# Quarter products for six gated blocks of an attention, gated layer and softmax-linear-unit kernel

## The chip, the cores and the metric

The kernel runs on one core of a Trainium2 chip. The core has engines that work beside each other, each through its own queue in program order: TensorE (PE; its weight loads are listed apart as PEld), VectorE (DVE), ScalarE (ACT), GpSimd (POOL) and SyncE (SP), which here issues nearly all transfers between the device memory and the on-chip memory. An engine waits for another through semaphores. The metric is device time of one execution in microseconds (us), the median of several runs.

## The reference

```python
def _moe_ref(x, w1, w2, w3, w_out):          # x: 1792 tokens x 768, from attention
    a = x @ w1                               # 768 x 1024
    b = x @ w2
    h = a * b @ w3                           # 1024 x 1024
    return (h @ w_out).astype(np.float32)    # 1024 x 768

def _moe2_ref(x, w_in, w_out, g_ln):
    h = x @ w_in                             # 768 x 1024
    e = np.exp(h - np.max(h, axis=-1, keepdims=True))
    sm = e / (np.sum(e, axis=-1, keepdims=True) + 1e-09)
    solu = h * sm
    ln = (solu - mean(solu)) / np.sqrt(var(solu) + 1e-06) * g_ln
    return (ln @ w_out).astype(np.float32)   # 1024 x 768
```

Ahead of these stands attention over 4 sequences, 12 heads, 448 positions of width 64, whose scores are capped by a tanh. Its output, laid out as 1792 tokens of width 768, is the x of the gated layer.

## The kernel before

Numbers are held as two parts, a high one and a low one of reduced precision, and each product is made as three (`THREE`: high by high, high by low, low by high). Splitting a tile means a cast on ScalarE for the high part ("a<-s", "ws<-ws" in the rows) and a subtraction on VectorE for the low part.

The work has three stages. Attention goes over 24 pairs of heads. Beside it run the folding of weights (w3, w_out and w_in are multiplied into one matrix W of 1024 x 1024, since nothing stands between them) and the first gated blocks. The gated stage makes, for each block f of 128 of the 1024 columns of w1 and w2 and each of the four sequences b (448 tokens), two banks of 128 x 448 with 6 x 3 matmuls each (L981); one is copied by ScalarE (L338), and VectorE multiplies the other with it (`evict`, L1002) into "abs", which SyncE stores (`ab_dr`). It goes in two passes: all eight blocks for sequences 0 and 1, then all eight for sequences 2 and 3 (`PASSES`). For the second pass six of the eight blocks' weights are fetched again, 1.5 MB each (`plan_again`, L790, "wt<-w_dr"), from a copy in the device memory.

Stage 3 multiplies the gated result with W in seven rounds of two token tiles, takes the softmax-like part, and multiplies with wout2 in seven more. Each round is one Strassen-Winograd step: with halves of both operands, seven products (`product`, L1202; order 1, 2, 6, 7, 5, 4, 3) instead of eight, each of 12 matmuls of 512 columns (384 for wout2). Products 1, 6, 5 and 3 go to a bank "u", 2 to "y", 7 and 4 to "v"; 6 starts anew in "u", 5 and 3 add to it, 4 adds to "v". Between them the banks are copied by ScalarE (`kept`, L1206: "p", "u") or summed by VectorE (`added`, L1228). The operands of the products are sums of quarters ("s", "a0_1" to "a0_7" for round 0) and of W's quarters ("ws1" to "ws7"), whose sums are formed on VectorE in the gated stage (`plan_sums`, L866 to L869: "t") and stored (`tw_dr`, `tg_dr` for wout2).

What sets the order: up to the end of the gated stage a planner (`Order`, `Ahead`) places the work beside TensorE's by costs written into each step and by the order in which items were planned; wout2's conversions (`plan_last`: L326, L329, L332 on VectorE, the gain L910 on ScalarE, a store) were planned behind the first pass's blocks. In stage 3 the order is written out: `plan(r, j, ...)` lists what stands behind product j of round r. Either way each engine then runs its list in order. `first_operands` (L962, L963) makes the operands of stage 3's first products in the second pass.

Of the kernel before, what the change touches and what calls it, by code (L numbers as in the profile page):

```python
# [18 lines left out]
P = 128  # L19
# [13 lines left out]
PLAIN, XR, LEAN = 6, 5, 1000.0  # L33
# [208 lines left out]
def attention_moe_solu(ctx: ExitStack, tc: tile.TileContext, q, k, v, cap, w12, w3t, wo, win, wout2, g_ln, out):  # L242
# [40 lines left out]
    right, left = [], []  # L283
    at = opened(right, "at", "right")
# [221 lines left out]

    def values(n):
# [127 lines left out]

    STAGE1, HALFWAY = 4 * NC * NF * 3, NC * NF * 3
# [123 lines left out]
    wt, xs, rb, fin = {}, {}, {}, set()  # L760
# [5 lines left out]
    def slot12(f, i):  # L766
        if i == 0:
            p = place["wt"] if f >= NF and (f - NF) % 3 == 2 else res[0]
            wt[f] = p.tile([P, 2, 2 * DM], F32R, tag="wres", bufs=1 if p is not res[0] else 2, name=f"wt{f}")
        return wt[f][:, 0, i * HALF:(i + 1) * HALF], wt[f][:, 1, i * HALF:(i + 1) * HALF]  # L770

    def free12(f):

        if f == NF + 2:
            return "wt" in place
        before = f - 2 if f < NF + 2 else f - 3
        return pos[0] >= STAGE1 and (f < 2 or (before, PASSES[before // NF][-1]) in fin)
# [8 lines left out]
    def plan_again(f):  # L786
        def load():
            for i in range(3):
                slot12(f, i)
            sync.dma_start(out=raw(wt[f]), in_=w12_dr[block(f)])  # L790
        for i in range(3):
            ahead.add(("w", f, i), load if i == 0 else (lambda: None), list, list, None, there12(f))

    def place_x(b, c):

        n = b * NC + c
        if n < W3 or n >= 2 * W3:
            return w3p.tile([P, 2, HALF], F32R, tag="w3", bufs=W3, name=f"xs{b}_{c}")[:, :, :S]
        return place["x"].tile([P, 2, S], F32R, tag="xs", bufs=W3, name=f"xs{b}_{c}")

    def free_x(b, part):
        if b == 0:
            return pos[0] >= STAGE1 + (HALFWAY if part else 0)
        return (pos[0] >= STAGE1 + HALFWAY if (b, part) == (1, 0) else "x" in place) and (b < 3 or (NF - 1, 0) in fin)

    def plan_x(b, parts=range(NPAIR // 2)):
        for part in parts:
# [17 lines left out]
            def scale(i=i, part=part, one=one):  # L825
                dve.scalar_tensor_tensor(xr[b, part], xr[b, part], one[0], rb.pop(i), ALU.mult, ALU.mult)
# [4 lines left out]
            def rest(part=part):  # L831
                x, steps = xr.pop((b, part)), []
                for i in range(2):
                    to = xs[b, 2 * part + i]
                    steps.append(("any", 1, copying(S), None, lambda e, to=to, i=i: cast(to[:, 0], x[:, i], e)))
                for i in range(2):
                    to = xs[b, 2 * part + i]
                    steps.append(("dve", 2, 560, 680, lambda to=to, i=i: low(to[:, 0], to[:, 1], x[:, i])))
# [19 lines left out]

    def plan_sums(kind, dr, t_dr, i_, part, n):
# [3 lines left out]
        def rest():  # L863
            b = lands.pop(i).rearrange("p (g h n) -> p g h n", g=2, h=2)
            t = [place["ts"].tile([P, HALF], F32, tag="ts", bufs=5, name=f"t{i}_{m}")[:, :2 * n].rearrange("p (t n) -> p t n", t=2) for m in range(2)]
            dve.tensor_tensor(t[0][:, 0], b[:, 0, 1], b[:, 0, 0], ALU.subtract)  # L866
            dve.tensor_tensor(t[0][:, 1], b[:, 1, 1], t[0][:, 0], ALU.subtract)
            dve.tensor_tensor(t[1][:, 0], b[:, 1, 1], b[:, 0, 1], ALU.subtract)
            dve.tensor_tensor(t[1][:, 1], b[:, 1, 0], t[0][:, 1], ALU.subtract)  # L869
            for m in range(2):  # L870
                sync.dma_start(out=t_dr[2 * m:2 * m + 2, :, i_, part * n:(part + 1) * n].rearrange("t p n -> p t n"), in_=t[m])
# [20 lines left out]
    def fifth(m):  # L892
        if m not in place["ws"]:
            close(right, 1)
            place["w5"] = opened(right, "ws5", "right")
            place["ws"][m] = place["w5"].tile([P, 2, NF // 2, HALF], F32R, tag=f"w{m}", name=f"ws{m}")
        return place["ws"][m]

    def plan_block(m, part):
        there = since((lambda: "ws" in place) if m != EARLY[4] else (lambda: (NF + 5, PASSES[1][1]) in fin and ("tg", NF // 2 - 1, 1) in ahead.done))  # L900
        ahead.add(("f", m, part), lambda: block_load(m, part, W4, tw_dr, fifth(m)), list,
                  lambda: [("none", 0, 0, 0, lambda: block_split(ws[m], part))], None, there)

    def plan_last(f):
        for u in range(2):
            i, slots, t = len(ahead.items), [], []

            def gain(i=i, t=t):
                t.append(early.tile([P, DM // 2], F32, tag="wg", bufs=2, name=f"wg{f}_{u}"))
                act.activation(t[0], cvs.pop(i), AF.Copy, scale=gt[:, f:f + 1])  # L910

            def rest(slots=slots, gain=gain, u=u, t=t):
                return [("act", 1, 460, 640, gain), ("none", 0, 0, 0, lambda: ring["cv"].give(slots[0], order.time)), ("sp", 0, 450, 5000, lambda: sync.dma_start(out=wg_dr[f, u], in_=t[0]))]
            ahead.add(("g", f, u), lambda i=i, u=u: landing(i, wout2[f, u].bitcast(U32), DM, U32), lambda i=i, slots=slots: convert(i, DM // 2, slots), rest, lambda: ring["cv"].when() if order.live else 0.0, None, ("sp", 450, 6000))
# [12 lines left out]
    plan_again(NF + 2)  # L927
# [3 lines left out]
    for f in range(NF):  # L931
        if f >= 3:
            plan_again(NF + f)
        if f < 4:
            for part in range(2):
                plan_block(EARLY[f], part)
    for i_ in range(NF // 2):
        for part in range(2):
            plan_sums("tg", G4, tg_dr, i_, part, DM // 4)
    for part in range(2):  # L940
        plan_block(EARLY[4], part)
# [23 lines left out]
    ahead.add("a0", load_first, list, lambda: [("none", 0, 0, 0, first_operands)], None, since(lambda: (NF + 2, PASSES[1][0]) in fin))  # L965

    def gated():
        pp = {}

        def products(f, b, cs):  # L970
            at_ = f - 2 if f in (NF, NF + 1) else f
            for i in range(2):
                for c in cs:
                    for m, (u, e) in enumerate(THREE):
                        begins = c == 0 and m == 0
                        yield 201, [("w", at_, (i * NC + c) // 4), ("x", b, c // 2), *(bank("f") if begins else [])]
                        if begins:
                            tag = "o" if "ws" in place and (i if b < 3 or f >= NF + 2 else f % 2) else "f"
# [7 lines left out]
            if cs[-1] < NC - 1:  # L986
                return
# [380 lines left out]
    def load_wg(m):  # L1368
        wg[m] = (wsp if m in EARLY[:4] else place["w5"] if m in EARLY else wsl).tile([P, 2, NF // 2, HALF], F32R, tag=f"w{m}", name=f"wg{m}")[:, :, :, :DM // 2]
        block_load(m, None, G4, tg_dr, wg[m])  # L1370

    def parts(t, part):
        return (t[:, i, rows(part), :] for i in range(2))

    def high_w(t, m, part=None):
        hi, lo = parts(t[m], part)
        act.copy(hi, raw(lo))

    def low_w(t, m, part=None):
        hi, lo = parts(t[m], part)  # L1380
        dve.tensor_tensor(lo, raw(lo), raw(hi), ALU.subtract)  # L1381

    def plan(r, j, *entries):
        for f, *args in entries:
            side.setdefault((r, j), []).append(lambda f=f, args=args: f(*args))
# [9 lines left out]

    plan(0, 0, (load_late, 4), (load_late, 3), (load, 1, 0), (load, 1, 1), (begun_sums,))
    plan(0, 1, (high, 0, 7))
    plan(0, 2, (high, 0, 5), (low, 0, 7), (high_w, ws, 4, 0))
    plan(0, 3, (high, 0, 4), (sum4, 0), (low, 0, 5), (low_w, ws, 4, 0), (high_w, ws, 4, 1))
# [125 lines left out]
```

## Time and profile before

| | us |
|---|---|
| median of 3 runs (785.34 to 785.66) | 785.48 |
| the profiled execution | 786.16 |
| its span, first to last instruction | 784.4 |
| TensorE busy in it | 777.3 |
| VectorE busy | 551.5 |
| ScalarE busy | 422.5 |
| GpSimd busy | 54.5 |

The rows further below are of the profiled execution. "Idle before" a row is the time in which its engine stood, and the name behind the arrow is what ended it. The chain of waits follows the work that ended last back to the start; where it runs on TensorE without a gap, TensorE sets the time there. "Landing" of a transfer is from its issue to its end. The granted clock is TensorE's, as a share of full speed; it is 1.000 over the span.

### The profile page before, as it was taken

What the parts mean: (1) busy time and instruction counts of PE and PEld (TensorE: products, weight loads), DVE (VectorE), ACT (ScalarE), POOL (GpSimd) and SP (SyncE); (2) the same over time, 40 slices, a digit from 0 to 9 for tenths busy, and PEclk for the clock granted to TensorE, in tenths of its full rate; (3) what the DMA queues carried; (4) which work ended last, traced back from release to release, by engine and by line L of the source; (5) the groups of instructions that cost most, each with busy time, mean ns of one, the idle gap of its engine ahead of it and who ended that gap; (6) DMA issues with size and microseconds to landing.
All of it is one profiled execution on the core that took longest, in us unless ns stands there. A gap on an engine that the chain in (4) does not pass through costs nothing.

```text
span 784.4 us, 11179 instructions
## 1 busy us (share of the span) xinstructions
PE 777.3 (99%) x4010; PEld 621.2 (79%) x4010; DVE 551.5 (70%) x998; ACT 422.5 (54%) x614; POOL 54.5 (7%) x106
## 2 busy tenths in 40 slices
PE   9999999999999999999999999999999999999998
PEld 6556666876856676767999999998788888999998
DVE  6896695789984478955785743441886668978972
ACT  6786767347467866672332311121576666845642
POOL 0111000100110111100000000000011111100000
PEclk9999999999999999999999999999999999999999
DMA  8867375677972374738888999962553345997332
GB/s 288 248 222 233 115 230 160 191 246 245 295 245 80 104 256 157 247 140 306 323 279 229 338 383 359 355 227 95 156 162 108 107 106 135 291 181 151 105 107 81
DMA packets 145559, 162.45 MB, mean 207 GB/s; under 512 B 66084, under 2 KB 116448, under 8 KB 143968
## 3 DMA queue, kind: packets, MB, share of 16 engines
q1 hardware_dynamic: 142768, 155.91, 62.0%
q0 software_dynamic: 2592, 5.73, 3.1%
q8 instruction: 31, 0.51, 0.3%
q14 instruction: 24, 0.20, 0.1%
q10 hardware_dynamic: 144, 0.10, 0.0%
HBM read 114.04 MB, written 47.53 MB: 206 GB/s over the span
## 4 chain that ended last, share of the span: by engine, by line
PE 97%; ACT 1%; DVE 1%; issue 0%; DVEq 0%
PE ab L981 30%; PE u L1202 17%; PE o L513 10%; PE f L749 9%; PE v L1202 8%; PE f L733 8%; PE sc L440 6%; PE y L1202 4%; PE n L513 2%; PE sc L436 2%; PE idle L1119 1%; PE idle L1162 1%; ACT p L458 1%; ACT sc L453 1%; DVE ws L1381 0%
## 5 line engine op out<-in xcount | busy, mean ns | idle before, releaser
L981 PE MATMUL ab<-xs,wt 128*128 128x448 f32 x1152 | 234.0, 363 | 0.0
L981 PEld LDWEIGHTS ab<-xs,wt 128*128 128x128 f32 x1152 | 215.4, 187 | 18.9 <-issue 4.5
L453 ACT ACTIVATE sc<-sc,small 128x896 f32<-128x896 f32 (+1 forms) x96 | 82.8, 887 | 52.9 <-PE sc L440 46.9
L458 ACT ACTIVATE p<-sc,small 128x896 f32<-128x896 f32 (+1 forms) x96 | 84.9, 920 | 0.6
L1202 PE MATMUL u<-ws,a 128*128 128x512 f32 x336 | 80.3, 390 | 1.1 <-DVE abs L1002 0.8
L513 PE MATMUL o<-p,vd 128*64 128x448 f32 x384 | 77.5, 545 | 0.0
L1202 PEld LDWEIGHTS u<-ws,a 128*128 128x128 f32 x336 | 62.9, 188 | 15.0 <-DVE abs L1002 1.1
L733 PE MATMUL f<-w,w_o 128*128 128x512 f32 x288 | 70.7, 396 | 0.0
L749 PE MATMUL f<-w_i,w 128*128 128x512 f32 x288 | 68.6, 393 | 0.1
L733 PEld LDWEIGHTS f<-w,w_o 128*128 128x128 f32 x288 | 53.2, 188 | 16.3 <-issue 3.4
L749 PEld LDWEIGHTS f<-w_i,w 128*128 128x128 f32 x288 | 53.4, 188 | 14.5 <-issue 3.0
L1202 PE MATMUL u<-wg,a 128*128 128x384 f32 x336 | 62.0, 334 | 0.0
L1202 PEld LDWEIGHTS u<-wg,a 128*128 128x128 f32 x336 | 58.6, 188 | 0.3 <-DVE a L1333 0.3
L338 ACT COPY a<-ab 128x448 f32<-128x448 f32 x32 | 17.0, 530 | 77.6 <-PE ab L981 71.7
L513 PEld LDWEIGHTS o<-p,vd 128*64 128x64 f32 x384 | 25.4, 136 | 41.2 <-issue 40.2
L332 DVE SCALAR_TENSOR_TENSOR cv<-ld,cv 128x512 uint32<-128x512 uint32 (+1 forms) x80 | 52.2, 659 | 0.8
L329 DVE SCALAR_TENSOR_TENSOR cv<-ld,cv 128x512 uint32<-128x512 uint32 (+1 forms) x80 | 51.9, 658 | 0.9
L1329 ACT CAST a<-s 128x512 fp32r<-128x512 f32 (+1 forms) x42 | 31.3, 754 | 31.2 <-DVE s L1351 17.0
L479 DVE TENSOR_TENSOR s<-p,p 128x896 f32<-128x896 f32 x18 | 19.6, 1090 | 38.0 <-PE n L513 21.2
L326 DVE TENSOR_SCALAR cv<-ld 128x512 uint32<-128x512 uint32 (+1 forms) x80 | 32.2, 407 | 17.8 <-DMA ld<-in_wout 9.8
L1202 PE MATMUL v<-ws,a 128*128 128x512 f32 x168 | 40.4, 389 | 0.0
L1333 DVE TENSOR_TENSOR a<-s,a 128x512 fp32r<-128x512 f32 (+1 forms) x42 | 35.5, 851 | 5.8 <-ACT a L1329 5.7
(148 smaller groups left out, 1064.6 us busy)
## 6 DMA issues: line engine op xcount, KB each, us to landing
ld<-in_w SPq DMA_DIRECT2D x24, 512.0 KB, 5.4
w_dr<-wt SPq DMA_DIRECT2D x6, 1536.0 KB, 6.6
wt<-w_dr SPq DMA_DIRECT2D x6, 1536.0 KB, 8.7
ld<-in_w3t SPq DMA_DIRECT2D x16, 512.0 KB, 4.6
w_dr<-e SPq DMA_DIRECT2D x28, 256.0 KB, 3.3
ab_dr<-abs SPq DMA_DIRECT2D x32, 224.0 KB, 4.1
ldx<-ab_dr SPq DMA_DIRECT2D x14, 512.0 KB, 4.3
c_dr<-h SPq DMA_DIRECT2D x14, 512.0 KB, 2.8
```

Source lines behind the costliest of these rows:

```text
L326: dve.tensor_scalar(d[1], d[0][:, :, 1], 5, 2, ALU.logical_shift_left, ALU.logical_shift_right)
L329: dve.scalar_tensor_tensor(d[1], d[0][:, :, 1], 0xC0000000, d[1], ALU.bitwise_and, ALU.bitwise_or)
L332: dve.scalar_tensor_tensor(d[1], d[0][:, :, 0], 29, d[1], ALU.logical_shift_right, ALU.bitwise_or)
L440: pe.matmul(sc[:, j, :S], keys[rows], qq[rows, :], start=(m == 0), stop=(m == len(terms) - 1))
L453: act.activation(sc[:, :w, :S], sc[:, :w, :S], AF.Tanh, scale=qscale)
L458: act.activation(p, sc[:, :w, :S], AF.Exp, scale=capt)
L513: pe.matmul(dst[i * width:(i + 1) * width, :S], weights, moving, start=first, stop=stop)
L733: pe.matmul(banks_[c][0], lw[:, a], fw["3", h, g][:, e], start=begins, stop=(g == NF - 1 and m == 2))
L749: pe.matmul(begun_[m_][0], w34[m_][:, a, c, :], rw[:, e], start=(c == 0 and m == 0), stop=(c == NC - 1 and m == 2))
L981: pe.matmul(pp[f, b, i][0][:, :S], w[:, u], xs[b, c][:, e], start=begins, stop=(c == NC - 1 and m == 2))
L1202: pe.matmul(banks[g], a[r][m][:, p, k * P:(k + 1) * P], b[m][:, e, k, :], start=(first and k == 0 and i == 0), stop=(k == NF // 2 - 1 and ...
L1333: dve.tensor_tensor(lo, source(r, m), raw(hi), ALU.subtract)
```

## The change

Six blocks of the second pass (f = 0 to 5; 6 and 7 stay as they were and come first) are made like stage 3's rounds. A block's weights for w1 and w2 (768 x 256 in all) and the tokens of sequences 2 and 3 are cut into halves along the depth of 768, the columns (w1 and w2) and the tokens (sequences 2 and 3). Seven quarter products of 9 matmuls of 128 x 448 make what took 72 matmuls. For each set, as such a block is called here, VectorE forms four sums of weight quarters (`combine`, `combine_low`), high and low parts are split again (`high12`, `low12`), and the banks are kept and summed (`keep12`, `plus`, `finish`). Sums of the tokens are formed once (`two_three`, `one_four`). The order of the six sets is written out by `plan(n, j, ...)`, with the loads of later sets (`load_set`), half of the sums for wout2 (`tg_half`), the loads for stage 3 and `first_operands` at fixed places. wout2's conversions of blocks 0 to 5 are planned among the weights that are folded during attention. ws6 and ws7 are loaded in the last set, and ws5 in stage 3's first round.

```diff
@@ wout2's conversions
+    for f in range(3):
+        plan_last(f)
     plan_3(1, *range(NF))
+    for f in range(3, 6):
+        plan_last(f)
...
-        if f >= 4:
-            plan_last(2 * f - 8)
-            plan_last(2 * f - 7)
+        if f >= 6:
+            plan_last(f)
@@ the second pass
-        for f in range(NF + 2, 2 * NF):
-            for b in PASSES[1]:
-                yield from products(f, b, every)
+            for b in (first, last):
+                yield from products(NF + f, b, every)
...
+        for half in (slice(2 * QUARTER, None), slice(0, 2 * QUARTER)):
+            sync.dma_start(out=raw(sets[n][0][:, :, half]), in_=w12_dr[n][:, :, half])
...
+    def multiply(n, j):
+        m = ORDER[j]
+        g, begins = {1: "u", 2: "y", 6: "u", 7: "v", 5: "u", 4: "v", 3: "u"}[m], m in (1, 2, 7)
...
+        for c in range(NC // 2):
+            for i, (u, e) in enumerate(THREE):
+                pe.matmul(pu[g], w[:, u, c * P:(c + 1) * P], moved(m, c)[:, e], ...)
...
+    def finish(n, j):
+        if j in (0, 2, 3):
+            keep12(n, *{0: ("u", "p1"), 2: ("u", "u2"), 3: ("v", "p7")}[j])
+        elif j == 1:
+            plus("y", "p1")
+        elif j == 4:
+            plus("u", "p7")
+        elif j == 5:
+            plus("v", "u2")
+            dve.tensor_tensor(keeps["u2"], keeps["u2"], keeps["p1"], ALU.mult)
+            given(n, PASSES[1][0], "u2")
+        else:
+            dve.tensor_tensor(keeps["p7"], pu["u"], keeps["p7"], ALU.mult)
+            given(n, PASSES[1][1], "p7")
...
+        if n + 1 < AGAIN:
+            plan(n, 2, (combine, n + 1, 5))
+            plan(n, 3, (combine_low, n + 1, 5), (combine, n + 1, 7))
+            plan(n, 4, (combine_low, n + 1, 7), (combine, n + 1, 6))
...
+        if n + 2 < AGAIN:
+            plan(n, 6, (load_set, n + 2))
...
+        if n < 2 * NF // 2 - EARLY_G:
+            plan(n, 0, (tg_load, EARLY_G + n))
+            plan(n, 3, (tg_half, EARLY_G + n, 0))
+            plan(n, 4, (tg_half, EARLY_G + n, 1))
+    plan(LATER - 1, 0, (load_first,))
+    plan(LATER, 0, (last_sets,), (load_ws, EARLY[2]), (load_ws, EARLY[3]))
+    plan(LATER, 3, (first_operands,))
@@ stage 3, round 0
-    plan(0, 1, (high, 0, 7))
-    plan(0, 2, (high, 0, 5), (low, 0, 7), (high_w, ws, 4, 0))
+    plan(0, 1, (high, 0, 7), (low, 0, 7), (high, 0, 5), (low, 0, 5), (high_w, ws, 5, 0))
+    plan(0, 2, (low_w, ws, 5, 0), (high_w, ws, 5, 1), (high_w, ws, 4, 0))
```

VectorE in the second pass, before: what stands between the multiplies of one block (abs_13, for sequences 2 and 3) and behind them.

```order
645 L1002 TENSOR_TENSOR abs_13_2_4792<-ab1_13_2_4767,a_13_2_4765 128x448
646 L866 TENSOR_TENSOR t120_0_4921<-ld120_4848 128x192
647 L867 TENSOR_TENSOR t120_0_4921<-ld120_4848,t120_0_4921 128x192
648 L868 TENSOR_TENSOR t120_1_4922<-ld120_4848 128x192
649 L869 TENSOR_TENSOR t120_1_4922<-ld120_4848,t120_0_4921 128x192
650 L1002 TENSOR_TENSOR abs_13_3_4879<-ab1_13_3_4838,a_13_3_4836 128x448
```

The four operations of 192 columns are sums for wout2. Now, in set 3 (q4_4 holds weights of set 4, s5, s7 and s63 are its sums; us3 and vs3 are the banks of set 3, p7s3 and u2s3 what is kept of them):

```order
743 L974 TENSOR_TENSOR s7_4_4997<-q4_4_4934 128x384
744 L975 TENSOR_TENSOR s7l_4_4998<-q4_4_4934 128x384
745 L889 TENSOR_TENSOR ttg7_0_5001<-ldtg7_4953 128x192
746 L890 TENSOR_TENSOR ttg7_0_5001<-ldtg7_4953,ttg7_0_5001 128x192
747 L987 TENSOR_TENSOR s7_4_4997<-s7_4_4997,s7l_4_4998 128x384
748 L982 TENSOR_TENSOR s63_4_5017<-s5_4_4980,q4_4_4934 128x384
749 L892 TENSOR_TENSOR ttg7_1_5019<-ldtg7_4953 128x192
750 L893 TENSOR_TENSOR ttg7_1_5019<-ldtg7_4953,ttg7_0_5001 128x192
751 L1316 TENSOR_TENSOR p7s3_5005<-us3_4940,p7s3_5005 128x448
752 L987 TENSOR_TENSOR s63_4_5017<-s63_4_5017,q4_4_4934 128x384
753 L1316 TENSOR_TENSOR u2s3_4984<-vs3_4986,u2s3_4984 128x448
754 L1330 TENSOR_TENSOR u2s3_4984<-u2s3_4984,p1s3_4956 128x448
```

The sums of the next set's weights and those for wout2 stand ahead of the sum of bank us3 (row 751), and the first result (row 754) behind it.

ScalarE where the gated stage ends and stage 3 begins, before (p1_0 and u2_0 are the kept banks of round 0, a0_5 the operand of product 5):

```order
404 L338 COPY a_15_3_5091<-ab0_15_3_5072 128x448
405 L1206 COPY p1_0_5161<-u_0_5138 128x512
406 L1329 CAST a0_7_5176<-s2_0_5159 128x512
407 L1329 CAST a0_5_5194<-s1_0_4996 128x512
408 L1377 CAST ws4_5131<-ws4_5131 128x1024
409 L1206 COPY u2_0_5198<-u_0_5138 128x512
```

And now, from the last set's keep of its fourth product:

```order
444 L340 CAST a0_6_5234<-s2_0_5225 128x512
445 L1313 COPY p7s5_5237<-vs5_5214 128x448
446 L1350 CAST ws6_5184<-ws6_5184 128x1024 x2
447 L1350 CAST ws7_5185<-ws7_5185 128x1024 x2
448 L1424 COPY p1_0_5330<-u_0_5301 128x512
449 L1547 CAST a0_7_5345<-s2_0_5328 128x512
450 L1547 CAST a0_5_5348<-s1_0_5224 128x512
451 L1350 CAST ws5_5314<-ws5_5314 128x1024 x2
452 L1350 CAST ws4_5294<-ws4_5294 128x1024
453 L1424 COPY u2_0_5371<-u_0_5301 128x512
```

The cast of a0_6 moved ahead of the keep p7s5, and two casts of ws5 stand between a0_5 and the keep u2_0. The tile a0_5 is now in a ring of buffers in which it lies over a0_6.

## Rows read from the trace of the kernel before

**Rows 1.** The page's busy times, share of the span and instructions.

```profile
PE 777.3 (99%) x4010; PEld 621.2 (79%) x4010; DVE 551.5 (70%) x998; ACT 422.5 (54%) x614; POOL 54.5 (7%) x106
```

**Rows 2.** The chain that ended last, by engine and by line.

```profile
PE 97%; ACT 1%; DVE 1%; issue 0%; DVEq 0%
PE ab L981 30%; PE u L1202 17%; PE o L513 10%; PE f L749 9%; PE v L1202 8%; PE f L733 8%; PE sc L440 6%; PE y L1202 4%; PE n L513 2%; PE sc L436 2%; PE idle L1119 1%; PE idle L1162 1%; ACT p L458 1%; ACT sc L453 1%; DVE ws L1381 0%
```

**Rows 3.** TensorE's waits, all: total us, times, longest us.

```profile
PE idle L1119 <- DVE zero L1115: 1.4, 1, 1.4
PE u L1202 <- DVE abs L1002: 0.8, 1, 0.8
PE v L1202 <- ACT p L1206: 0.5, 1, 0.5
PE sc L440 <- ACT p L458: 0.4, 1, 0.4
PE u L1202 <- DVE a L1333: 0.3, 1, 0.3
```

**Rows 4.** The chain in order of time: start us, us, instructions.

```profile
362.67 180.03 PE ab L981 x899
...
569.05 2.72 PE u L1202 x12
```

**Rows 5.** Busy PE, PEld, DVE, ACT, POOL per stretch; clock, DMA share, GB/s.

```profile
50.00:100.00 50.00, 50.00 (x287) 30.26 (x286) 35.68 (x67) 36.67 (x52) 5.92 (x10) 1.00 0.60 192
100.00:150.00 50.00, 50.00 (x261) 33.70 (x260) 36.88 (x67) 31.99 (x44) 3.96 (x6) 1.00 0.60 187
...
450.00:500.00 50.00, 50.00 (x252) 46.86 (x251) 22.29 (x49) 8.36 (x12) 0.00 (x0) 1.00 1.04 373
500.00:550.00 50.00, 49.23 (x242) 44.99 (x241) 15.33 (x30) 8.73 (x15) 0.00 (x0) 1.00 0.60 197
```

**Rows 6.** VectorE's and ScalarE's groups by shape: busy us, mean ns.

```profile
L866 DVE TENSOR_TENSOR t<-ld 128x192 f32<-128x192 f32 x8 | 2.8, 354 | 4.3 <-DMA ld<-wg_dr 2.4 <-DMA tg_dr<-t 1.9
...
L1225 DVE TENSOR_TENSOR o<-y,p 128x384 f32<-128x384 f32 x7 | 3.9, 552 | 4.2 <-issue 3.9 <-PE y L1202 0.3
...
L1002 DVE TENSOR_TENSOR abs<-ab,a 128x448 f32<-128x448 f32 x16 | 10.0, 622 | 24.4 <-PE ab L981 14.8 <-issue 5.3 <-DMA ab_dr<-abs 4.3
...
L347 DVE TENSOR_TENSOR ws<-ws 128x1024 fp32r<-128x1024 f32 x10 | 12.2, 1222 | 6.8 <-ACT ws L338 6.8
...
L332 DVE SCALAR_TENSOR_TENSOR cv<-ld,cv 128x384 uint32<-128x384 uint32 x16 | 8.8, 555 | 0.3
L329 DVE SCALAR_TENSOR_TENSOR cv<-ld,cv 128x384 uint32<-128x384 uint32 x16 | 8.8, 554 | 0.3
L326 DVE TENSOR_SCALAR cv<-ld 128x384 uint32<-128x384 uint32 x16 | 5.6, 356 | 10.0 <-DMA ld<-in_wout 9.8 <-ACT wg L910 0.2
...
L910 ACT ACTIVATE wg<-cv,small x16: 599/617/620, 359.6 to 423.2; 128x384 f32<-128x384 f32 x16
```

**Rows 7.** The six loads of 1.5 MB (L790): durations of issue, then landing.

```profile
L790 SPq DMA_DIRECT2D wt<-w_dr x6: 332/360/587, 433.4 to 501.2; - x6
...
DMA to landing us min/median/max: 6.6/8.7/13.8
```

**Rows 8.** Timeline at the gated stage's end: start us, us, instruction, idle before.

```profile
518.60 1.29 DVE L347 TENSOR_TENSOR a<-ldx,a 128x512 fp32r<-128x512 f32 x2 [2.81 <-ACT a L338]
...
522.37 0.69 DVE L963 TENSOR_TENSOR s<-s,ldx 128x512 f32<-128x512 f32 x1
...
543.45 3.06 PE L1202 MATMUL u<-ws,a 128*128 128x512 f32 x12 [0.77 <-DVE abs L1002]
...
549.35 0.62 ACT L1329 CAST a<-s 128x512 fp32r<-128x512 f32 x1 [1.69 <-PE y L1202]
...
555.90 2.00 ACT L1377 CAST ws<-ws 128x1024 fp32r<-128x1024 f32 x2
...
563.77 2.56 PE L1202 MATMUL u<-ws,a 128*128 128x512 f32 x10 [0.28 <-DVE a L1333]
```

More of the change, by code (lines that the diff above doesn't have):

```diff
@@ L634, in passed, with plan_last, gain, rest @@
         return h * STAGE1 // 2 + STAGE1 // 3 + 24 * (g // 2) + 18 + 6 * (g % 2)
+    def plan_last(f):
+        for u in range(2):
+            i, slots, t = len(ahead.items), [], []
+            def gain(i=i, t=t):
+                t.append(early.tile([P, DM // 2], F32, tag="wg", bufs=2, name=f"wg{f}_{u}"))
+                act.activation(t[0], cvs.pop(i), AF.Copy, scale=gt[:, f:f + 1])
+            def rest(slots=slots, gain=gain, u=u, t=t):
+                return [("act", 1, 460, 640, gain), ("none", 0, 0, 0, lambda: ring["cv"].give(slots[0], order.time)), ("sp", 0, 450, 5000, lambda: sync.dma_start(out=wg_dr[f, u], in_=t[0]))]
+            ahead.add(("g", f, u), lambda i=i, u=u: landing(i, wout2[f, u].bitcast(U32), DM, U32), lambda i=i, slots=slots: convert(i, DM // 2, slots), rest, lambda: ring["cv"].when() if order.live else 0.0, None, ("sp", 450, 6000))
     STAGE1, HALFWAY = 4 * NC * NF * 3, NC * NF * 3
@@ L784, in plan_w @@
             plan64(("w", f, i), w12[f, i], HALF, lambda i=i: slot12(f, i), there12(f))
[L786 to L792, printed above, removed]
     def place_x(b, c):
         n = b * NC + c
-        if n < W3 or n >= 2 * W3:
+        if b == 3 and c < 2:
+            return place["set"].tile([P, 2, S], F32R, tag="xb", bufs=2, name=f"xs{b}_{c}")
+        if b == 3:
+            return place["xe"].tile([P, 2, S], F32R, tag="xe", bufs=4, name=f"xs{b}_{c}")
+        if n < W3:
             return w3p.tile([P, 2, HALF], F32R, tag="w3", bufs=W3, name=f"xs{b}_{c}")[:, :, :S]
@@ L890, in block_split, with second @@
         split(hi, lo, raw(lo))
[L892 to L897, printed above, removed]
+    def second(m):
+        if m not in ws:
+            ws[m] = both_.tile([P, 2, NF // 2, HALF], F32R, tag="many", name=f"ws{m}")
+        return ws[m]
     def plan_block(m, part):
-        there = since((lambda: "ws" in place) if m != EARLY[4] else (lambda: (NF + 5, PASSES[1][1]) in fin and ("tg", NF // 2 - 1, 1) in ahead.done))
-        ahead.add(("f", m, part), lambda: block_load(m, part, W4, tw_dr, fifth(m)), list,
+        there = since(lambda: "ws" in place)
+        ahead.add(("f", m, part), lambda: block_load(m, part, W4, tw_dr, second(m)), list,
                   lambda: [("none", 0, 0, 0, lambda: block_split(ws[m], part))], None, there)
[L904 to L914, printed above, removed]
     plan_w(0)
@@ new lines, in tokens, with third, halves, plan_plain @@
+    def tokens(m, c):
+        p = place["x"] if m == 1 else w3p
+        tx[m, c] = p.tile([P, 2, S if m == 1 else HALF], F32R, tag="xs" if m == 1 else "w3", bufs=W3, name=f"t{m}_{c}")[:, :, :S]
+    def third(j):
+        return whole[(NC // 2 + j) // 2][(NC // 2 + j) % 2]
+    def halves(x):
+        return raw(x[:, 0]), raw(x[:, 1])
+    def plan_plain(key, do, test, load=lambda: None):
+        ahead.add(key, load, list, lambda: [("none", 0, 0, 0, do)], None, since(test))
+    def two_three(c):
+        if c == 0:
+            for m in (2, 3):
+                for i in range(NC // 2):
+                    tokens(m, i)
+        t2, t3, (h, l), t = tx[2, c], tx[3, c], halves(xs[2, c]), whole[c // 2][c % 2]
+        dve.tensor_tensor(t, third(c), t, ALU.subtract)
+        split(t3[:, 0], t3[:, 1], t)
+        dve.tensor_tensor(t, t, h, ALU.add)
+        dve.tensor_tensor(t, t, l, ALU.add)
@@ L928, in attention_moe_solu @@
+    plan_plain("set0", lambda: None, lambda: "set" in place, lambda: load_set(0))
     for i_ in range(NF // 2):
@@ L1178, in attention_moe_solu @@
+    assert not side
     close(left)
```

240 lines of the change are left out of this document (180 added, 60 removed).

## Prediction

> **What bounds the kernel now.** I read the busy totals first, then the chain of waits, then the list of TensorE's waits, and last the stretch that is rewritten. TensorE is busy for 99% of the span, VectorE for 70% [rows 1], and 97% of the chain that ended last is TensorE's own work [rows 2]. All its waits together are some 3 us, and the longest inside the work is 0.8 us, where stage 3's first product waits for the last gated multiply [rows 3]. So time falls only by what TensorE is spared, and rises by every wait that is new. The largest group of the chain is the gated products [rows 2]. Behind attention they run alone: 899 matmuls of 448 columns in 180.03 us, which is 0.2003 us each [rows 4]. This is the stretch that is rewritten. In it VectorE is far from full (22.29 of 50 us) and the DMA engines are full: share 1.04 at 373 GB/s [rows 5]. One group of twelve 512-column matmuls takes 2.72 us in stage 3 [rows 4].
>
> **What it removes.** Each of six blocks needs 7 quarter products of 9 matmuls, 63, where it had 72: 54 matmuls fewer, 54 x 0.2003 = 10.82 us. The 0.77 us before stage 3's first product [rows 8] goes too: that product's bank now waits for a sum of the last set that is done one product earlier; what is late next is counted at stage 3. I take off 0.77, and the 0.28 us wait before the second round [rows 8], to count it anew below. That makes -11.87 us.
>
> **What it moves ahead.** Twelve conversions of wout2 (three VectorE operations of 384 columns, a ScalarE gain, a load and a store each) run during attention. They cost VectorE 12 x (0.356 + 0.555 + 0.554) = 17.6 us and ScalarE 12 x 0.617 = 7.4 us [rows 6]. In 50 to 150 us VectorE is idle for 14.3 and 13.1 us of each 50 [rows 5], and TensorE's order in attention stays what it was but for some thirty rows that only split the same filling work elsewhere. I take 0. From below nothing can be gained, since TensorE hardly waits there (0.4 us for the scores [rows 3]). From above: a conversion ahead of a softmax sum holds it by 1.47 us, and two such places where no filling work is ready make 3 us; that end is kept for the range.
>
> **What it adds: VectorE inside the sets.** A set is 63 matmuls, 12.62 us; products end at 1.80, 3.61, 5.41, 7.21, 9.01, 10.82 and 12.62 us from its start. The fifth product's sum ("plus u") reads the bank into which the seventh product accumulates, so TensorE stands at 10.82 until it is done. Durations: 0.354 us for 192 columns, 0.552 for 384, 0.622 for 448, 1.22 for 1024 [rows 6]. In a row they overlap: two of 512 last 1.29 [rows 8] where one has 0.69, so 0.08 is saved, which gives about 0.28, 0.475 and 0.54 from one start to the next, and 0.11 more where an operation reads the one before.
>
> Sets 1 to 3. The load of the set after the next is issued on SyncE behind the store of the set's first result, whose multiply comes about 2.2 us after the sixth product's end. Its halves leave about 0.4 and 0.85 us into the next set. A load of the same 1.5 MB block takes at least 6.6 us to land [rows 7]; from the second half that is 7.4. Between it and the end of "plus u" VectorE has four operations of 384 columns, four of 192 (stage 3's sums) and the sum itself: 4 x 0.475 + 1.23 + 0.62 = 3.8 with the dependent ones, so 11.3 against 10.82: 0.5 us each, 1.5 in all. The loads of the rows landed in 6.6 to 13.8, median 8.7 [rows 7]. I take 6.6, because the rows near the median were issued where the DMA engines were full [rows 5], while a set now moves one load of 1.57 MB, two results of 0.23 MB and 0.79 MB of sums in 12.62 us, 223 GB/s (worked out). With 8.7 us the same walk gives 13.4, that is 2.6 in the first set and some 0.45 less in those behind it, since then the store ahead of the load leaves earlier against the set's end: about 2.3 each.
>
> Set 0 has its load long before, but two lows of 1024 columns (1.14 each) come into VectorE's row; behind the second product's sum, which ends at 4.2 us, stand eight operations of 384 columns, four of 192, one such low and "plus u": 4.2 + 3.8 + 1.3 + 1.1 + 0.6, with 0.2 for dependent ones 11.2 to 11.3. That is 0.5 us, 0 to 2 by where the two lows fall. Set 4 has no sums of 192: 7.4 + 0.1 + 4 x 0.475 + 0.62 = 10.0, no wait. Set 5: on ScalarE the keep of the fourth product's bank stands behind the cast of a0_6, which waits on VectorE for two lows and two sums (the first keep ends at 5.5, casts to 6.4, lows and sums at 0.6 to 0.7 each [rows 8] to 9.2, cast to 9.8, keep to 10.3). The sixth product accumulates into that bank from 9.01: 1.3 us.
>
> **What it adds: stage 3's first round.** Count from its start. In the kernel before, the cast of a0_5 waited for the second product (1.69 us behind "y" [rows 8]). Now that tile lies where a0_6 lies, which the third product reads until 3 x 2.72 = 8.16. Behind it on ScalarE stand two casts of ws5, one of ws4 (2.00 for two [rows 8]) and only then the keep of the third bank: 8.2 + 0.55 + 2.0 + 1.0 + 0.5 = 12.2 to 12.3. The fifth product accumulates into that bank from 10.88: 1.3 us. Then the last product waits about 0.36 for ws3's second low, and the next round 0.75 for its first low: 2.4 together.
>
> **The sum.** -11.87 + 0.5 + 1.5 + 1.3 + 2.4 = -6.2 us. Against the profiled execution, 786.16 us with a span of 784.4, that is 780.0 and 778.2; it ran 0.7 over the median, so the median of 785.48 becomes 779.3.
>
> In the Trainium skill, "DMA: Bandwidth & Descriptors", section "Anatomy of one DMA — SWDGE (gpsimd) path", a transfer takes 2.0 us and its bytes at 436 GB/s, for GpSimd's path; an estimate by it for 1.57 MB is 5.6 us. The trace has no such load under 6.6 [rows 7], so the trace is slower than the rule; by the rule the sets 1 to 3 would not wait and the sum would be -7.7.
>
> **Rivals.** (1) Fewer waits: the loads land by 6.9 us, or casts and lows keep ahead of the walk, which supposes every operation as late as its row allows. For it: VectorE's 70% [rows 1]. Against it: one instruction out of place holds an in-order engine. Without the waits of sets 0 to 3 and half of the others: -11.87 + 1.9, about 775.5.
>
> (2) The load sets the pace of the sets, the side on which nothing is gained. Place: the second half's landing before "plus u" in sets 1 to 4. Price: with 8.7 us, 3 x 1.8 more in sets 1 to 3 and 1.1 in set 4, 785.8 us; each further microsecond costs about 4. From about 8.1 us of landing on nothing is gained that can be told, and from 9.0 the kernel is slower. For it: the median [rows 7]. Against it: the share of the DMA engines above.
>
> (3) The conversions in attention are late: +3, 782.3.
>
> (4) TensorE's clock falls behind the new waits. In the rows the granted clock is 1.00 in each stretch, the 2.4 GHz level, also in the one with the 0.77 us wait [rows 5, 8]. If one product of 1.80 us ran at half of it behind each of five waits, that would be 5 x 1.80 = 9 more, 788.3.
>
> The Trainium skill, "TensorE: Matmul & The Clock Gate", Part 1, says that the clock drops to 1.2 GHz when the engine has been idle; no stretch of this trace shows the lower level, so it bears out none of (4).
>
> **How the numbers follow.** Forecast 0.52 (its own range 777.3 to 781.7), (1) 0.20, (3) 0.09, (2) 0.15, (4) 0.04. What this measurement tells from no change is 0.2%, 783.9 to 787.05. Forecast, (1), (3) and a third of (2) are faster: 0.52 + 0.20 + 0.09 + 0.05 = 0.86. Same is 0.06, the middle of (2). Slower is its rest of 0.04 and (4), 0.08. The range 775.5 to 784.3 leaves out some 0.08 below and 0.14 above.
>
> **What would show it.** Right: 1,098 gated matmuls at 0.200 us; in TensorE's list of waits, VectorE's sum of 448 columns at about 0.5 us in four sets, ScalarE's keep at about 1.3 us once in the last set, another keep at 1.3 in stage 3's first round, and nothing new in attention. Landings of the set loads near 6.6 us bear out the walk; near 8.7, rival (2). Wrong: waits in every set of over 1 us, a new wait in attention, a clock under 1.00, or no waits at all.

## The result and the profile after

The changed kernel takes 794.84 us (median, 792.48 to 796.04 in 4 runs) beside 785.41 us (785.10 to 785.66, 4 runs) for the kernel before: ratio 1.0114, 95% interval 1.0094 to 1.0134. It is slower by 1.1%; 779.3 with a range to 784.3 was predicted, so sign and size are wrong.

The profiled execution of the changed kernel took 795.62 us, its span is 793.8. First the page's busy times, which answer to [rows 1]:

```profile
PE 773.2 (97%) x3956; PEld 611.9 (77%) x3956; DVE 615.9 (78%) x1129; ACT 442.2 (56%) x659; POOL 55.1 (7%) x106
```

54 matmuls are gone (4010 to 3956), yet TensorE's busy time fell by only 4.1 us, and the span grew by 9.4. Then TensorE's waits, which answer to [rows 3] (engine, line, what was waited for: total us, times, longest):

```profile
PE us L1309 <- ACT p1s L1313: 8.2, 1, 8.2
PE us L1309 <- DVE p7s L1316: 2.3, 3, 0.8
PE vs L1309 <- ACT p7s L1313: 1.9, 2, 1.3
PE idle L1225 <- DVE zero L1221: 1.4, 1, 1.4
PE u L1420 <- ACT u L1424: 1.3, 1, 1.3
PE v L1420 <- ACT p L1424: 0.8, 1, 0.8
```

L1309 are the matmuls of the sets, L1313 ScalarE's keeps of their banks ("p1s", "u2s", "p7s"), L1316 VectorE's sums with a bank, and L1420 the products of stage 3. One wait stands out: 8.2 us, once, for the keep of a first product's bank. The description of the kernel before has it that product 6 starts bank "u" anew. In the program only products 1, 2 and 7 start a bank, in stage 3 as in the sets (`begins`); product 6 adds to product 1, so product 1 must have been copied out first. That is why TensorE waits here. Most of the other waits are where the forecast had them. The timeline of TensorE gives the place and the length of each set (start us, us, instructions, idle before):

```profile
458.42 1.96 PE L1309 MATMUL us<-xs,q 128*128 128x448 f32 x9
...
470.37 3.73 PE L1309 MATMUL us<-t,q 128*128 128x448 f32 x9 [8.19 <-ACT p1s L1313]
...
479.77 2.56 PE L1309 MATMUL us<-xs,q 128*128 128x448 f32 x12
...
493.56 3.88 PE L1309 MATMUL us<-xs,q 128*128 128x448 f32 x18 [0.75 <-DVE p7s L1316]
...
507.42 3.88 PE L1309 MATMUL us<-xs,q 128*128 128x448 f32 x18 [0.78 <-DVE p7s L1316]
...
521.97 3.88 PE L1309 MATMUL us<-xs,q 128*128 128x448 f32 x18 [0.76 <-DVE p7s L1316]
...
534.73 3.76 PE L1309 MATMUL us<-xs,q 128*128 128x448 f32 x18
...
546.97 2.08 PE L1309 MATMUL vs<-t,q 128*128 128x448 f32 x9 [1.28 <-ACT p7s L1313]
...
550.69 2.96 PE L1420 MATMUL u<-ws,a 128*128 128x512 f32 x12
```

In the rows of 12 and 18 matmuls the next set begins behind the first nine, 1.80 us in. So the sets last 23.15, 13.79, 13.86, 14.55, 12.76 and 14.16 us, where 12.62 was the length without a wait. In set 0 the wait is not all: the two products behind it take 3.73 and 2.23 us by the chain below, where 1.80 is usual. The windows show why (start:end, then PE, PEld, DVE, ACT, POOL busy, granted clock, DMA share, GB/s):

```profile
460.00:470.00 10.00, 2.18 (x11) 1.70 (x10) 3.12 (x10) 1.16 (x2) 0.00 (x0) 0.73 1.06 390
470.00:480.00 10.00, 9.63 (x38) 8.81 (x39) 8.94 (x18) 3.51 (x7) 0.00 (x0) 0.76 0.43 148
480.00:490.00 10.00, 10.00 (x52) 9.37 (x51) 7.37 (x15) 1.85 (x4) 0.00 (x0) 1.00 0.72 238
```

The granted clock fell to 0.73 and 0.76 around the wait, that is, part of the stretch ran at 1.2 GHz instead of 2.4; from 480 us on it is full again. The two slow products took about 2.4 us more than 1.80 each, which is also part of why TensorE's busy time fell so little. While TensorE stood the DMA engines were full (share 1.06).

The chain of waits through this place (start us, us, what):

```profile
455.49 6.88 DMA q<-w_dr
462.40 0.03 issue
462.43 6.34 DMA ws<-w_dr
...
468.84 0.04 ACT ws L340
468.89 0.91 issue
469.80 0.54 ACT p1s L1313
470.33 0.04 issue
470.37 3.73 PE us L1309 x9
474.10 2.23 PE vs L1309 x9
```

It reads: SyncE issued the load of ws2 (for stage 3) only when the first half of set 1's weights ("q") had landed; that load took 6.34 us; ScalarE's cast of ws2 waited for it, and the keep that TensorE needed stood behind the cast. The cast itself is for stage 3's second product, some 85 us later.

Where the 9.4 us of span come from, forecast in brackets: attention's end +2.1 (0); removed products -10.8 (-10.8); the wait before stage 3 -0.8 (-0.8); set 0 +10.5 (0.5); sets 1 to 3 +4.3 (1.5); sets 4 and 5 +1.7 (1.3); stage 3 +2.2 (2.1): it lasts 793.8 - 550.69 = 243.1 us, where it lasted 784.4 - 543.45 = 240.95 [rows 8]. Together +9.2. Attention's part is read behind the last pair, after (first fence) and before (second):

```profile
362.76 0.95 PE L523 MATMUL n<-s,ones 128*32 128x448 f32 x4
363.64 0.68 PE L1097 MATMUL ab<-xs,wt 128*128 128x448 f32 x2
364.25 0.94 PE L523 MATMUL n<-s,ones 128*32 128x448 f32 x4
365.13 1.07 PE L1097 MATMUL ab<-xs,wt 128*128 128x448 f32 x4
```

```profile
361.71 0.96 PE L513 MATMUL n<-s,ones 128*32 128x448 f32 x8
362.60 1.68 PE L981 MATMUL ab<-xs,wt 128*128 128x448 f32 x7
```

The last sums come 1.05 us later, and the group of eight is split in two groups of four that take as long each; two gated matmuls stand between them. The unbroken run of gated matmuls starts 2.53 us later (365.13 against 362.60) with two more done, 2.1 us net.

### The profile page after: what moved, and what is told of

It is laid out like the page before. It is cut to its first block, busy times and chain, and to the rows that moved or that the text cites. A ratio compares the mean times of both kernels' runs of the same rounds, so it can differ in the third digit from the quotient of the medians.

```text
span 793.8 us, 11282 instructions
## 1 busy us (share of the span) xinstructions
PE 773.2 (97%) x3956; PEld 611.9 (77%) x3956; DVE 615.9 (78%) x1129; ACT 442.2 (56%) x659; POOL 55.1 (7%) x106
## 4 chain that ended last, share of the span: by engine, by line
PE 71%; DMA 11%; DVE 9%; ACT 5%; issue 3%; SPq 1%; DVEq 0%; ACTq 0%
PE u L1420 14%; PE o L523 9%; PE f L775 8%; PE v L1420 7%; PE ab L1097 7%; PE f L759 6%; PE sc L442 6%; PE y L1420 4%; PE us L1309 3%; DMA ldtg<-wg_dr 2%; PE n L523 2%; PE sc L438 2%; DMA ws<-w_dr 2%; DMA wg_dr<-wg 1%; PE vs L1309 1%
## 5 line engine op out<-in xcount | busy, mean ns | idle before, releaser
L1097 PE MATMUL ab<-xs,wt 128*128 128x448 f32 x720 | 148.0, 364 | 0.0
L1097 PEld LDWEIGHTS ab<-xs,wt 128*128 128x128 f32 x720 | 134.3, 188 | 14.4 <-issue 5.2
L1420 PE MATMUL u<-ws,a 128*128 128x512 f32 x336 | 80.6, 391 | 1.8 <-ACT u L1424 1.3
L1420 PEld LDWEIGHTS u<-ws,a 128*128 128x128 f32 x336 | 62.8, 188 | 16.1 <-ACT u L1424 1.8
L1420 PE MATMUL u<-wg,a 128*128 128x384 f32 x336 | 62.1, 335 | 0.0
L1420 PEld LDWEIGHTS u<-wg,a 128*128 128x128 f32 x336 | 58.5, 188 | 0.5 <-DVE a L1551 0.2
L1420 PE MATMUL v<-ws,a 128*128 128x512 f32 x168 | 40.4, 389 | 0.0
L1420 PEld LDWEIGHTS v<-ws,a 128*128 128x128 f32 x168 | 31.5, 188 | 6.6
```

The source lines that it names most:

```text
L1097: pe.matmul(pp[f, b, i][0][:, :S], w[:, u], xs[b, c][:, e], start=begins, stop=(c == NC - 1 and m == 2))
L1420: pe.matmul(banks[g], a[r][m][:, p, k * P:(k + 1) * P], b[m][:, e, k, :], start=(first and k == 0 and i == 0), stop=(k == NF // 2 - 1 and ...
```

## The experiments

Each is a change of the changed kernel unless said otherwise; times are medians, ratios to the kernel before run on the same chip, with the 95% interval. Lengths of sets and waits are of the one profiled execution of each kernel. The changed kernel's interval, 1.0094 to 1.0134, is the one to compare with. "Block 9" is the second block of the second pass, the last one made in the old way, just ahead of set 0 (blocks are counted through both passes).

**First group: who holds set 0.** e1 leaves ws2's load in its place and moves its casts and lows to the last set; e2 moves two of the four sums for wout2 from ahead of set 0 into the sets; e3 does both; e4 puts the conversions back.

```diff
e1:
-            plan_block(EARLY[1], part)
+            plan_plain(("f", EARLY[1], part), lambda: None, ..., lambda part=part: block_load(EARLY[1], part, ...))
+    plan(LATER, 0, (high_w, ws, EARLY[1], 0), (high_w, ws, EARLY[1], 1))
+    plan(LATER, 1, (low_w, ws, EARLY[1], 0), (low_w, ws, EARLY[1], 1))
e2:
-    EARLY_G = 4
+    EARLY_G = 2
+    plan(LATER - 1, 1, (tg_load, NF - 1))
+    plan(LATER - 1, 5, (tg_half, NF - 1, 0))
+    plan(LATER - 1, 6, (tg_half, NF - 1, 1))
e4:
-    for f in range(3):
-        plan_last(f)
...
-        if f >= 6:
-            plan_last(f)
+        if f >= 4:
+            plan_last(2 * f - 8)
+            plan_last(2 * f - 7)
```

Expected of e1:

> ws2 is still loaded where it was, but its casts and lows stand in the last set, so ScalarE's keep of set 0's first bank no longer stands behind a cast that waits for that load. Theory A (ScalarE held by ws2's load is what costs set 0 its 10.5 us): set 0 falls from 23.2 to about 13 us, the clock does not drop, time near 784.5 us. Theory B (VectorE, held by the stores of its sums, is as late by itself: the multiply of block 9 that frees a bank for set 0 ends at 468.9, 10.5 us into the set): set 0 still lasts some 18 to 19 us, time near 790 us.

Measured 793.28 us, ratio 1.0097 (1.0080 to 1.0114). The longest of TensorE's waits in e1:

```profile
PE vs L1309 <- DVE abs L1116: 4.8, 1, 4.8
```

and its chain ahead of that wait:

```profile
458.49 7.46 DMA tg_dr<-t
...
467.79 0.54 DVE abs L1116
```

The 8.2 us wait is gone and set 0 waits 4.8 us for VectorE's multiply of block 9, which stands behind sums for wout2 that wait for a store of such sums to land. So ScalarE's cast was the holder that ended last, and not the only one: theory A alone falls, and B holds as to the next holder, though not in its number: set 0 lasts 20.2 us, where B had 18 to 19. Of the 2.9 us that set 0 gave back, 2.2 went again in stage 3 (245.3 us), and e1's interval overlaps that of the changed kernel, so a gain in time is not shown.

Expected of e2:

> Two of the four sums for wout2 that stand ahead of set 0 move into the sets (one in set 4, and the last one behind that set's sixth product); ws2's split stays ahead of set 0. Theory A: the cast of ws2 still holds the keep; its load leaves some 3 us earlier, so set 0's wait falls from 8.2 to about 5 us and the time to about 791. Theory B: VectorE is not held before set 0, so most goes, time near 785.

Measured 799.24 us, 1.0173 (1.0156 to 1.0190). The wait for p1s stays (7.9 us): block 9's multiply now ends at 458.9 us, in time, and ws2's load leaves 2.5 us earlier, but both casts of ws2 now stand ahead of the keep, and the second starts only at 468.19. Two of the moved sums cost waits of 0.6 us each in sets 4 and 5. Neither theory gave this: taking the second holder alone away gains nothing, as it hides behind the first.

Expected of e3:

> Both edits. Either theory: set 0 near 13 us, time 782 to 785 us. If both theories hold in part, this gains clearly more than e1 and e2 each.

Measured 796.42 us, 1.0137 (1.0122 to 1.0153): both theories fail. Its chain in set 0:

```profile
455.02 8.73 DMA ldtg<-wg_dr
...
463.82 5.78 DMA ab_dr<-abs
...
469.67 0.54 ACT u2s L1313
470.21 0.04 issue
470.26 3.09 PE us L1309 x9
```

Here is a third holder: the keep u2s goes into a tile whose store ("ab_dr<-abs") must have landed. SyncE issued that store late, when a transfer issued at 455.02 had landed after 8.73 us, and the store took 5.78. TensorE waited 4.4 us. Set 0 did get shorter, 18.9 us. The time did not. In set 5 the moved casts of ws2 stand ahead of the keep p1s, behind another cast that a moved sum holds up on VectorE; TensorE waits 2.4 us for that keep, the granted clock is 0.83 from 535 to 545 us, and the set lasts 18.4 us, where it lasted 14.2.

Expected of e4:

> wout2's twelve conversions stand where they stood before the change, in the gated stage; the quarter products stay. If the conversions cost attention its 2.1 us, attention ends as in the kernel before (o of the last pair 1.05 us earlier, the piece behind it 1.1 earlier) and the gated stage carries 17.6 us more of VectorE: 793 if that is covered, 796 or more if VectorE is then later still ahead of set 0 (theory B).

Measured 805.08 us, 1.0254 (1.0234 to 1.0274), 10 us worse than with the conversions in attention:

```profile
PE us L1306 <- DVE p7s L1313: 11.2, 3, 9.9
PE ab L1094 <- ACT wt L340: 4.7, 2, 2.5
```

VectorE is then so late that set 0 waits 9.9 us for the sum ahead of its last product. But set 0 lasts 25.5 us, only 2.4 more than in the changed kernel; the larger loss lies ahead of it, where the unbroken run of gated matmuls takes 101.9 us (467 of them) and not 93.3 (465), with the waits for ScalarE's "wt" and a granted clock of 0.83 from 400 to 410 us. So in this order the twelve conversions cannot all stay in the gated stage. And attention then ends nearly as in the kernel before, with the last sums in one piece and the run from 362.91 us, 0.3 us later:

```profile
362.02 0.96 PE L523 MATMUL n<-s,ones 128*32 128x448 f32 x8
```

**Second group: the queue, and each part alone.** e5 issues the loads of sets 1 to 5 from GpSimd; e6 is e5 with e1; e7 is e6 with the two orders on ScalarE; e8 is the kernel before with only the conversions moved.

```diff
e5:
-            sync.dma_start(out=raw(sets[n][0][:, :, half]), ...)
+            (pool if n else sync).dma_start(out=raw(sets[n][0][:, :, half]), ...)
e7:
-        begin(6, s2)
+        begun["later"] = lambda: begin(6, s2)
+    plan(LATER, 4, (sixth_operand,))
-    plan(0, 1, (high, 0, 7), (low, 0, 7), (high, 0, 5), (low, 0, 5), (high_w, ws, 5, 0))
+    plan(0, 1, (high, 0, 7), (low, 0, 7), (high_w, ws, 5, 0), (high_w, ws, 5, 1), (high, 0, 5), (low, 0, 5))
```

Expected of e5:

> The changed kernel, but the weight loads of sets 1 to 5 are issued from GpSimd's queue and not from SyncE's. Theory C (the root of set 0's loss is SyncE: behind the two halves of set 1's load it stands until a transfer issued eight before has landed, so ws2's load, the stores of the sums and those of block 9's result leave late): ws2's load leaves at about 458.4 instead of 462.4 us, set 0's wait for the keep falls from 8.2 to about 3 us, and sets 1 to 3 lose their 0.75 us waits since their loads leave earlier: about 786 us. Theory D (the DMA engines themselves are full, whatever queue issues): stores and ws2 land as late as before, set 0 stays above 20 us, 793 to 796.

Measured 791.76 us, 1.0065 (1.0047 to 1.0083): between C and D, and clear of the changed kernel. The wait for p1s falls to 4.6 us, and a wait of 1.8 us for block 9's multiply comes in its place, so set 0 still lasts 22.1 us, 1.0 less. Most of the gain is in sets 1 to 3, as C had it for them: 12.8, 12.7 and 13.8 us, together 3.0 less.

Expected of e6:

> As the run before, and ws2's casts and lows stand in the last set. Theory C: neither ScalarE nor VectorE is held in set 0, which lasts about 13 us at the full clock: 781 to 783 us. Theory D: set 0 near 19 us as with ws2 moved alone, 790 or more.

Measured 790.90 us, 1.0073 (1.0048 to 1.0097): C fails as the whole cause. Set 0 lasts 19.8 us, near what D had; the interval overlaps those of e5 and of e1.

Expected of e7:

> As the run before, and two orders on ScalarE: in the last set the cast of a0_6 stands behind the keep of the fourth product's bank (the 1.3 us wait there), and in stage 3's first round the casts of ws5 stand ahead of a0_5's and one of ws4's behind the third bank's keep (another 1.3 us). Theory C with those two waits as the forecast had them: 2 to 2.5 us under the run before, 779 to 780. If other operations are late in their place (a0_6 itself for stage 3's third product), under 1 us less.

Measured 789.83 us, 1.0046 (1.0031 to 1.0061), 1.1 under e6, with overlapping intervals. The last set's 1.3 us wait for p7s is gone, stage 3's became 0.7 and 0.3 us waits for lows on VectorE, and set 0 still waits 3.2 us for the keep u2s and lasts 19.1.

Expected of e8:

> The kernel before, with only wout2's twelve conversions moved into attention; no quarter products. If the conversions are what costs attention 2.1 us in the changed kernel, this runs at about 787.5 us, unless the gated stage, freed of 17.6 us of VectorE, gives something back; it has only a 0.8 us wait to give. If attention's 2.1 us come from the other edits (a buffer that moved), 785.5.

Measured 787.91 us, 1.0019 (1.0007 to 1.0032), that is 0.6 to 2.5 us. Its trace shows the same split of the last sums, and the run starts 2.00 us later with two more done, 1.6 us net:

```profile
363.73 0.95 PE L513 MATMUL n<-s,ones 128*32 128x448 f32 x4
364.60 7.68 PE L984 MATMUL ab<-xs,wt 128*128 128x448 f32 x37
```

**Third group: the sums for wout2 moved.** e9 is e7 with `EARLY_G = 2`, the sums of sets 1 to 4 behind the second product's sum, loaded a set ahead. e10 is e9 with the conversions planned behind w_in. e11 is e9 with the loads on SyncE.

```diff
e9:
+        for k in [EARLY_G + n] * (0 < n < LATER) + [NF - 1] * (n == 1):
+            plan(n, 2, (tg_half, k, 0), (tg_half, k, 1))
...
+        if n + 1 < LATER:
+            plan(n, 4, (tg_load, EARLY_G + n + 1))
e10:
+    for f in range(6):
+        plan_last(f)
     plan_w(0)
```

Expected of e9:

> As e7 (set loads on GpSimd, ws2's split in the last set, two orders on ScalarE), and two of the four early sums for wout2 move from ahead of set 0 into the sets; in sets 1 to 4 the sums stand where VectorE waits for the next set's load (behind the second product's sum), not ahead of the sum that the seventh product waits for. If VectorE's stops for store landings ahead of set 0 are what is left there (theory B with D), set 0 falls from about 17 to 13 us, the 0.8 and 1.6 us waits of sets 1 and 3 go: 781 to 783 us. If the stores of block 9's result alone hold the keep (landing behind other transfers), set 0 stays at 16 us or more: 787.

Measured 786.09 us, 1.0002 (0.9989 to 1.0015). This is clear of e7. Set 0's wait for the keep falls to 1.7 us and of the 0.8 and 1.6 us waits 0.5 is left, much as B with D had it; 3 us more than expected are left: set 0 lasts 15.4 us where 13 was expected, and block 9 waits 2.0 us for VectorE ahead of it.

Expected of e10:

> As e9, but the twelve conversions are planned behind w_in's parts, so that they run at some 200 to 290 us, where VectorE is busy for 28 of 50 us, and not at 50 to 200, where it is busy for 47. If attention's 1 to 2 us come from VectorE being late for a softmax sum in the full stretch, 1 to 2 us under e9; if the place doesn't matter, the same; if the first gated blocks' weights come late by it, over e9.

Measured 794.06 us, 1.0101 (1.0066 to 1.0137): over e9, as in the third of its cases. Attention's last sums start at 369.78 us, against 362.43 in e9. The emptier stretch was not free. That the first gated blocks' weights came late is not shown: the longest new wait of attention is one of 2.5 us in the folding of w_in, for a cast on ScalarE. Set 0 has no wait here and lasts 12.6 us; in its place block 9 waits 2.6 us for VectorE ahead of it, and set 1 waits 3.1 for its keep u2s.

Expected of e11:

> As e9, with the set loads on SyncE again. Theory C (SyncE's queue holds the stores behind the load): 3 to 5 us over e9. Theory D (only the DMA engines' load counts): the same as e9 within 1 us.

Measured 786.55 us, 1.0013 (1.0004 to 1.0022), within 0.5 us of e9, as D had it. But the queue still shows in the trace. Block 9 no longer waits for VectorE, and set 0 waits 2.9 us for the keep u2s, whose tile is free only when a store of block 9 has landed; SyncE issued that store when a transfer issued at 453.91 had landed:

```profile
453.91 7.82 DMA ldtg<-wg_dr
...
461.79 5.81 DMA ab_dr<-abs
...
467.66 0.54 ACT u2s L1317
```

So either queue costs about the same there, by different waits; it is not that the queue has no effect.

**Fourth group: the keeps apart.** e12 is e11 with the keep u2 in the ring that p1 uses, and an order on VectorE in stage 3; e13 is e12 with eight conversions in attention.

```diff
e12:
-        ... tag="a" if name == "p1" else "ab", bufs=2 ...
+        ... tag="ab" if name == "p7" else "a", bufs=2 ...
+    plan(0, 1, ..., (high_w, ws, 5, 1), (low_w, ws, 5, 0), (low_w, ws, 5, 1), (high, 0, 5), (low, 0, 5))
e13:
-    for f in range(3):
+    for f in range(2):
...
-        if f >= 6:
+        if f >= 4:
             plan_last(f)
```

Expected of e12:

> As e11, and two more holds taken away: the keep u2 of a set goes to the ring of two tiles that p1 uses, so that no keep waits for a store of the set before to land (the 2.9, 0.3 and 1.5 us waits for ScalarE's keeps in e11), and in stage 3's first round the lows of ws5 stand ahead of a0_5's low on VectorE (0.3 and 0.7 us waits, and a product that took 3.41 instead of 2.91 us). If those waits are what is left of the loss, 5 to 6 us under e11: 780 to 781 us. If the stores' landings come back at another place (the sum that frees the bank of block 9), 784.

Measured 783.68 us, 0.9969 (0.9956 to 0.9982): faster than the kernel before, by 0.3%. But set 0 is no shorter than in e11 (16.2 us against 15.7, with a lower clock behind its wait). What e12 gained beside e11 are set 3, from 14.3 to 12.7 us, where the keep p7s waited 1.5 us, and 1.5 us in stage 3. The longest of TensorE's waits:

```profile
PE vs L1313 <- ACT p7s L1317: 2.2, 1, 2.2
```

What is left in set 0 is once more a keep (p7s, one product later) behind the landing of a store, and the clock behind it:

```profile
463.19 5.74 DMA ab_dr<-abs
...
469.00 0.54 ACT p7s L1317
```

```profile
470.00:480.00 10.00, 10.00 (x44) 9.23 (x43) 6.21 (x13) 1.97 (x4) 0.00 (x0) 0.83 0.67 204
```

Expected of e13:

> As e12, but eight of the twelve conversions in attention, four back in the gated stage. If attention's cost goes with their number, its end comes 0.7 us earlier and the time is 780; if the gated stage's VectorE was the more precious place, its sums and stores are late again ahead of set 0 and the time is 783 or more.

Measured 782.28 us, 0.9964 (0.9946 to 0.9982). The intervals of e12 and e13 overlap, so what the four conversions do to the time is not told apart; set 0 waits 2.0 us for VectorE's sum there instead of the keep, and lasts 15.6. Attention is shorter: the last sums stand in one piece again,

```profile
358.14 0.96 PE L523 MATMUL n<-s,ones 128*32 128x448 f32 x8
```

and set 0 starts at 457.11 us, against 458.25 in e12. Both beat the kernels before and after.

## Why the prediction was wrong

The step that failed is this one: "Set 0 has its load long before, but two lows of 1024 columns (1.14 each) come into VectorE's row ... That is 0.5 us, 0 to 2 by where the two lows fall." It walked one engine, VectorE, and took everything that reaches set 0 from outside as there. It was 10.5 us. ScalarE's order was walked for the last set and for stage 3, but not for set 0, where a cast of ws2 stands ahead of the keep p1s, and SyncE's was walked without its stops. The runs show a pile of holders, each hiding the next: the cast (8.2 us in the profile after), VectorE's multiply of block 9 (4.8 in e1), the landing of a store (4.4 in e3), another store (2.2 in e12). Set 0 lasted 23.2 us in the changed kernel, 20.2 in e1, 18.9 in e3, 15.4 in e9 and 16.2 in e12, where 12.62 was forecast for the matmuls. So some 3 us of the loss stay in set 0 in the fastest kernels too, and the last step, below the kernel before, came from set 3 and stage 3.

In each of these chains the holder itself waits for a transfer: ws2's load (6.34 us), a store of sums (7.46), stores of block 9 (5.78 and 5.74). Ahead of set 0 the sums for W and wout2 and their stores, set 1's weights and ws2's load come together, at a DMA share of 1.06. Shown is that fewer sums there help together with the other edits (e9 against e7), and that issuing set 1's load elsewhere changes which wait ends last but shortens set 0 little where it can be compared (1.0 in e5, 0.4 in e6 against e1 and in e9 against e11, each read from one execution). That the full DMA engines are the common source is argued from this and from the landings, not shown by a run of its own. Not shown either is how much set 1's load alone does: its place ahead of set 0 was not changed.

The other steps, one by one. The pace was right: 465 ordinary matmuls from 365.13 to 458.42, 0.2006 us each, and set 4, with hardly a wait, 12.76 us. Sets 1 to 3: the mechanism was right, VectorE's "plus u" behind a load; the halves landed in 6.7 us (median of twelve), as taken from the low end of [rows 7]:

```profile
DMA to landing us min/median/max: 4.9/6.7/8.1
```

The size was off: 0.75 to 0.78 us of printed wait each, and 1.2 us of set length or more, because the row before a wait counts some 0.3 us that matmuls in a row overlap; set 3 had a wait of 0.6 us for the keep p7s besides. In set 1 VectorE starts on the second half 7.9 us into the set, where the walk had 7.4, and behind it waits 0.2 us more for another load, that of wout2's sums ("ldtg"), which the walk left out. Set 4, set 5 (1.28 us at p7s) and the first wait of stage 3 (1.34 us at the keep behind a0_5 and the two casts of ws5) came as walked. That stage 3's total fits, 2.2 us for 2.1, is partly luck: the next round waited 0.31 us for its low and not 0.75, and 0.3 us came later at another keep. Attention was costed at 0 with 3 us as the upper end, rival (3); it cost 2.1. That the conversions are the cause is shown by changing their number: net of the gated matmuls done, 0.3 us with none (e4), 0.9 with eight (e13), 1.6 with all twelve and no quarter products (e8). Each is one execution; the ten with the changed kernel's attention give 1.8 to 2.8. "Idle on average" was no cover: TensorE's filling work was ordered otherwise, and with twelve the last group of sums was split.

Rival (2), the load that sets the pace, named transfers, at the wrong place: it asked for a landing of 8.7 us between the sets, and the harm was done ahead of them, where set 1's first half took 6.9. Rival (4), the clock, came true in part: not behind the 0.6 to 1.3 us waits, where the granted clock stays 1.00, but behind the 8.2 us one, for 2.4 us. The Trainium skill, "TensorE: Matmul & The Clock Gate", Part 1, says that an idle engine falls back to 1.2 GHz; the trace agrees for that wait (0.73 and 0.76 of full).

## What to carry to other kernels

Where a change writes a new order, walk the first instance of a loop on every engine and queue, with what was left over from before; the start was worth 10 of the 15 us between forecast and time here. A wait that the trace names is the one that ended last: ask what would have ended second, since taking one holder away moves the wait to the next (8.2, 4.8, 4.4 and 2.2 us). Work for later, such as a cast for a product 85 us away, doesn't belong on an in-order engine ahead of what the next product needs, if it waits for a transfer. And compare the lengths of the parts, not only the total: e3 took 4.3 us out of set 0 and lost as much in set 5.

## What the runs showed of the hardware

The stores of 224 KB that held a keep of set 0 took 5.74 us (e12), 5.78 (e3) and 5.81 (e11) to land, at a DMA share of 0.94 to 0.99 from 460 to 470 us, and the keep that reuses the tile paid for it; the median of twenty such stores in the changed kernel is 4.3 us. A wait of 8.2 us went with a granted clock of 0.73 and 0.76 in the two stretches of 10 us around it. Shorter waits did not all act alike: 2.2 us in e12 and 2.0 in e13 were followed by 0.83 from 470 to 480 us, while 2.9 us in e11 and 2.0 in e9 left 1.00 in every stretch of 10 us from 460 to 480 and from 450 to 480; waits up to 1.3 us in the changed kernel did not lower it. So the length of a wait alone does not tell whether the clock falls. Four of the softmax sums ("n") in a row took 0.95 us, and eight 0.96, so splitting such a group of eight costs about 0.9 us more.
